# K, V, dK and dV transfers with token blocks dealt to the partitions 16 apart: what it does to a decode-attention forward and backward kernel

## The chip, the cores and the metric

The kernel runs on one core of a Trainium2 chip. The metric is the device time of one execution in microseconds (us). A run is labelled slow when it takes over 1.5% longer than the fastest run of the same kernel beside it, else fast; a kernel run only once has no label. Ratios below are the mean time of one kernel's fast runs over that of the other kernel's fast runs of the same rounds, so they are not quite the ratio of the medians that are quoted.

## The reference

One decode step of a conditioned block, with its gradients. The part that costs time is attention of one query over caches of 32 heads, 8192 tokens and 192 channels:

```python
scores = einsum('bhqd,bhkd->bhqk', q, k) * Dh ** -0.5    # k, v: (1, 32, 8192, 192), bfloat16
p = softmax(scores)
o = einsum('bhqk,bhkd->bhqd', p, v)
# then an output product and a small MLP; jax.vjp of it all returns
# dK and dV (each as large as K) and the smaller gradients
```

K, V, dK and dV are 100 MB each. Softmax and the sums over tokens do not care which token is where, as long as K, V, dK and dV agree.

## The kernel before

A head's 8192 tokens are spread over 128 partitions, 64 neighbouring tokens (a block of 24 KB in DRAM) to each. A transfer moves half a block per partition: 128 runs of 12,288 contiguous bytes, 1.5 MB.

```python
K_hd = [A_k_cache[0, h].rearrange("(p j) d -> p j d", p=P) for h in range(HQ)]   # P = 128, j = 64 tokens
# ... V_hd, dK_hd and dV_hd likewise

def load_k(h, t):                       # t: first or second half of each block; JH = 32
    kb = KB[(2 * h + t) % NKB]
    nc.sync.dma_start(out=kb, in_=K_hd[h][:, t * JH : (t + 1) * JH, :])
    return kb
# ... load_v is the same for V, issued from the same queue

def store(dst, s, src, lo=0, hi=JH):    # dV and dK, issued from the GpSimd queue
    h, t = ht(s)
    nc.gpsimd.dma_start(out=dst[h][:, t * JH + lo : t * JH + hi, :], in_=src[:, lo:hi, :])
```

There are two long stages. In the first, K and V of all heads are read for the forward pass. In the second, V is read again and dV and dK are written. Buffers let transfers run a few ahead of the compute.

## Time and profile before

| | before |
|---|---|
| time, median of 3 runs | 1442.29 us |
| first stage, up to the issue of the first dV store | 605.4 us |
| second stage, from there to the end | 840.5 us |
| load packets of 12,288 B, first stage: median, mean | 464, 481 ns |
| the same, second stage | 460, 485 ns |
| store packets of 12,288 B: median, mean | 460, 467 ns |

The packet rows come from the trace's record of every DMA packet. (Throughout, packets count as first stage from 50 us up to the first large store packet.) The stages are cut at the first start of the store line. The trace's view of it gives the least, median and longest duration in ns, then the first and the last start in us; the span (below) less 605.4 is the second stage.

```profile
L1113 POOL DMA_DIRECT2D out_dram<-KB x131: 531/533/590, 605.4 to 1432.6; - x131
```

The page of the kernel before gives the DMA engines by slices of one fortieth of the span: the mean busy share of the 16 DMA engines in tenths, and the GB/s that they moved.

```profile
span 1445.9 us, 30125 instructions
...
DMA  9999999999999996399999999999999999999997
GB/s 376 415 411 417 402 417 407 402 390 408 402 398 393 417 390 247 115 326 422 410 426 415 424 414 409 401 420 426 411 426 425 422 415 414 409 387 412 413 399 321
```

DMA is full except for a dip between the stages. The table by stretches of the kernel before, one stretch inside each stage. After the stretch and its length come the busy times (with the number of instructions in brackets) of TensorE, its weight loads, VectorE, ScalarE and GpSimd, then TensorE's granted clock, the DMA share and GB/s.

```profile
100.00:500.00 400.00, 368.48 (x5355) 283.78 (x5353) 378.44 (x353) 292.07 (x927) 6.46 (x12) 0.99 1.00 405
700.00:1400.00 700.00, 575.32 (x4280) 323.77 (x4277) 487.75 (x695) 413.56 (x580) 107.64 (x188) 0.55 1.01 414
```

In the first stage VectorE is busy 378 of 400 us while DMA is full (share 1.00): the two are balanced. Waits of the kernel before (us in total, times, longest):

```profile
DVE KB L882 <- DMA out_dram<-KB: 18.8, 10, 3.6
...
DVE prod L298 <- DMA KB<-in_A_k_cache_dram: 5.4, 2, 4.9
```

VectorE hardly waits for DMA. But there is no reserve: in the first stage a K load lands a median of about 1 us before its first use (worked out from landing and first reader). The DMA issues of the kernel before (count, size of each, median us from issue to landing):

```profile
out_dram<-KB POOLq DMA_DIRECT2D x125, 1536.0 KB, 15.8
VB<-in_A_v_cache_dram SPq DMA_DIRECT2D x123, 1536.0 KB, 11.4
KB<-in_A_k_cache_dram SPq DMA_DIRECT2D x64, 1536.0 KB, 10.2
```

### The profile page before, as it was taken

How to read it: one execution, taken by the hardware profiler on the slowest of the kernel's cores; microseconds unless marked ns; L12 is line 12 of the kernel's file. 1: busy time of each engine (PE TensorE's matmuls, PEld its weight loads, DVE VectorE, ACT ScalarE, POOL GpSimd, SP SyncE). 2: the span in 40 equal slices, each digit the busy share in tenths (PEclk: the TensorE clock that was granted, in tenths of full speed). 3: DMA queues.
4: the chain of work that ended last, by engine and by line, in shares of the span. 5: the costliest groups of instructions: out<-in, count | busy, mean ns of one | idle time of the engine just before them, and what ended most of it. 6: DMA issues, size and time to landing. Idle time of an engine off the chain costs nothing.

```text
span 1445.9 us, 30125 instructions
## 1 busy us (share of the span) xinstructions
PE 1213.8 (84%) x12639; PEld 793.1 (55%) x12639; DVE 1112.4 (77%) x1377; ACT 894.5 (62%) x1955; POOL 142.7 (10%) x256
## 2 busy tenths in 40 slices
PE   3899999999999989878888888889788878778874
PEld 1677777677777668644444444444444444444532
DVE  5999999999999986667676667676776667677674
ACT  0777767677777774555566565566565565555654
POOL 0000000000000000112111111111111011111111
PEclk8999999999999998565565555565555555555555
DMA  9999999999999996399999999999999999999997
GB/s 376 415 411 417 402 417 407 402 390 408 402 398 393 417 390 247 115 326 422 410 426 415 424 414 409 401 420 426 411 426 425 422 415 414 409 387 412 413 399 321
DMA packets 77703, 569.35 MB, mean 394 GB/s; under 512 B 8798, under 2 KB 26542, under 8 KB 37502
## 3 DMA queue, kind: packets, MB, share of 16 engines
q1 hardware_dynamic: 50842, 340.44, 58.7%
q0 software_dynamic: 26704, 226.97, 37.8%
q8 instruction: 99, 1.62, 0.4%
q14 instruction: 38, 0.31, 0.1%
q10 hardware_dynamic: 20, 0.00, 0.0%
HBM read 340.95 MB, written 226.43 MB: 392 GB/s over the span
## 4 chain that ended last, share of the span: by engine, by line
PE 32%; DVE 10%; DMA 6%; ACT 5%; issue 4%; POOL 1%; ACTq 0%; POOLq 0%; DVEq 0%
PE dot_ps L866 19%; DMA out_dram<-KB 6%; PE dv_ps L877 6%; DVE pq L857 5%; PE wT_ps L742 4%; ACT KB L878 2%; ACT wT L743 2%; DVE KB L882 1%; DVE dP L313 1%; PE do_ps L756 1%; DVE dq_junk L989 1%; ACT v_bc L961 0%; DVE dS L1161 0%; ACT do_r L757 0%; POOL er_b L700 0%
## 5 line engine op out<-in xcount | busy, mean ns | idle before, releaser
L878 ACT CAST KB<-dv_ps 128x768 bf16<-128x768 f32 x512 | 388.8, 804 | 275.6 <-PE dv_ps L877 273.1
L866 PE MATMUL dot_ps<-pq,ident_bf 128*128 128x256 bf16 x1536 | 365.2, 408 | 57.2 <-DVE pq L857 57.1
L357 ACT ACTIVATE vs<-VB,Ef 128x192 bf16<-128x192 bf16 x872 | 314.5, 442 | 0.0
L866 PEld LDWEIGHTS <-ident_bf 128*128 128x128 bf16 x1536 | 190.5, 135 | 185.7 <-issue 122.5
L877 PE MATMUL dv_ps<-do_r,er_b 1*128 1x192 bf16 x2048 | 222.3, 337 | 55.1 <-ACT KB L878 53.6
L882 DVE TENSOR_TENSOR KB<-qs_bc,dS 128x3072 bf16<-128x3072 bf16 x128 | 224.2, 1753 | 25.8 <-DMA out_dram<-KB 18.8
L857 DVE TENSOR_TENSOR pq<-VB,do_r 128x3072 bf16<-128x3072 bf16 x126 | 220.7, 1751 | 0.0
L298 DVE TENSOR_TENSOR prod<-KB,qs_bc 128x6144 bf16<-128x6144 bf16 x62 | 207.8, 3352 | 11.3 <-DMA KB<-in_A_k_cache_dram 5.4
L372 PE MATMUL mp<-vs,KB 128*128 128x193 bf16 x1984 | 194.3, 251 | 0.0
L877 PEld LDWEIGHTS <-er_b 1*128 1x128 bf16 x2048 | 92.2, 111 | 177.9 <-issue 173.7
L372 PEld LDWEIGHTS <-KB 128*128 128x128 bf16 x1984 | 174.6, 100 | 18.8 <-issue 4.5
L313 DVE TENSOR_REDUCE dP<-dot_ps 128x32 f32<-128x512 f32 x64 | 44.2, 691 | 145.4 <-PE dot_ps L866 145.4
L309 PE MATMUL dot_ps<-prod,ident_bf 128*128 128x512 bf16 x372 | 94.3, 391 | 44.2 <-DVE prod L303 44.2
L350 DVE TENSOR_TENSOR vs<-VB,E 128x1728 bf16<-128x1728 bf16 (+1 forms) x122 | 127.1, 1063 | 0.0
L303 DVE TENSOR_TENSOR prod<-prod 128x3072 bf16<-128x3072 bf16 x62 | 108.6, 1752 | 0.6
L377 PE MATMUL mp<-vs,KB 128*64 128x193 bf16 x1984 | 107.7, 252 | 0.0
L743 ACT COPY wT<-wT_ps 128x1024 bf16<-128x1024 bf16 x84 | 80.8, 962 | 43.0 <-PE wT_ps L742 42.8
L700 POOL DMA_DIRECT2D er_b<-eT_d x64 | 36.9, 577 | 590.1 <-PE dv_ps L877 579.2
L377 PEld LDWEIGHTS <-KB 128*64 128x64 bf16 x1984 | 80.7, 110 | 19.9 <-issue 19.9
L309 PEld LDWEIGHTS <-ident_bf 128*128 128x128 bf16 x372 | 34.8, 99 | 85.8 <-issue 57.8
L1113 POOL DMA_DIRECT2D out_dram<-KB x131 | 70.4, 542 | 46.4 <-ACT KB L878 38.5
L337 ACT ACTIVATE E<-S_h,negm 128x256 bf16<-128x256 f32 x31 | 15.7, 508 | 90.1 <-DVE negm L496 86.4
(269 smaller groups left out, 1005.0 us busy)
## 6 DMA issues: line engine op xcount, KB each, us to landing
out_dram<-KB POOLq DMA_DIRECT2D x125, 1536.0 KB, 15.8
VB<-in_A_v_cache_dram SPq DMA_DIRECT2D x123, 1536.0 KB, 11.4
KB<-in_A_k_cache_dram SPq DMA_DIRECT2D x64, 1536.0 KB, 10.2
wo_st<-in_A_wo_dram SPq DMA_DIRECT2D x31, 480.0 KB, 10.5
w_st<-in_A_wq_dram SPq DMA_DIRECT2D x12, 960.0 KB, 16.1
out_dram<-wo_st POOLq DMA_DIRECT2D x16, 480.0 KB, 19.0
out_dram<-w_st POOLq DMA_DIRECT2D x7, 960.0 KB, 17.7
w_st<-in_w_mod_dram SPq DMA_DIRECT2D x6, 960.0 KB, 15.2
```

Source lines behind the costliest of these rows:

```text
L298: V_.tensor_tensor(out=prod, in0=src, in1=vec[:, None, :].to_broadcast([P, JH, DH]), op=ALU.mult)
L309: T_.matmul(ps, lhsT=ident_bf, rhs=prod[:, :, k : k + TS], start=(k == 0), stop=(k == w - TS))
L350: V_.tensor_tensor(out=vs[:, 0:n, 0:DH].rearrange("p j (a b) -> p j a b", b=4), in0=v[:, v0 : v0 + n, :].rearrange("p j (a b) -> p j a b", ...
L357: A_.activation(out=vs[:, k, 0:DH], in_=v[:, v0 + k, :], func=ACT.Copy, scale=Ef[:, j0 + k : j0 + k + 1])
L372: T_.matmul(mp[:, 0:MW], lhsT=kb[:, j0 + k, 0:P], rhs=vs[:, k, 0:MW], start=(q == 0 and k == 0), stop=(z and k == JQ - 1), skip_group_chec ...
L377: T_.matmul(mp[p0 : p0 + 64, MO : MO + MW], lhsT=kb[:, j0 + k, P:DH], rhs=vs[:, k, 0:MW], start=False, stop=(z and k >= JQ - 2), skip_grou ...
L743: A_.copy(out=wT[:, x0 * P : (x0 + n) * P], in_=tp[:, 0 : n * P])
L857: V_.tensor_tensor(out=pq[:, q], in0=v_l[s][:, q * JQ : (q + 1) * JQ, :], in1=do_of(ht(s)[0])[:, None, :].to_broadcast([P, JQ, DH]), op=AL ...
L866: T_.matmul(ps[:, q * JQ : (q + 1) * JQ, :], lhsT=ident_bf, rhs=pq[:, q, :, k : k + TS], start=(k == 0), stop=(k == DH - TS), skip_group_c ...
L877: T_.matmul(ps[:, b, k * DH : (k + 1) * DH], lhsT=er[p0 : p0 + 1, 2 * m + k, :], rhs=doh[p0 : p0 + 1, :], start=True, stop=True)
L878: A_.copy(out=dV4[:, 2 * q : 2 * q + 2, m * PW : (m + 1) * PW], in_=ps[:, :, 0:PW])
L882: V_.tensor_tensor(out=dK[:, lo:hi, :].rearrange("p j (a b) -> p j a b", b=4), in0=qh.rearrange("p (a b) -> p a b", b=4)[:, None, :, :].to ...
```

## The change

Its intent: blocks of DRAM that are read (or written) at one moment should be neighbours, not far apart. (Which blocks are under way together no trace shows: its packet records name no engine and no partition.) Partition p = 8u + v now holds block 16v + u. The core of the diff (it defines `hd` twice, with no effect):

```diff
-    K_hd = [A_k_cache[0, h].rearrange("(p j) d -> p j d", p=P) for h in range(HQ)]
-    (V_hd, dK_hd, dV_hd likewise)
+    def hd(x):
+        return [x[0, h].rearrange("(v u j) d -> u v j d", v=8, u=16) for h in range(HQ)]
+
+    K_hd, V_hd, dK_hd, dV_hd = hd(A_k_cache), hd(A_v_cache), hd(out_2), hd(out_3)
...
-        nc.sync.dma_start(out=v, in_=V_hd[h][:, t * JH : (t + 1) * JH, :])
+        nc.sync.dma_start(out=v, in_=V_hd[h][:, :, t * JH : (t + 1) * JH, :])
(load_k and store likewise)
```

A K load's DRAM side, written [step, count] in elements, goes from `[[12288, 128], [1, 6144]]` to `[[12288, 16], [196608, 8], [1, 6144]]`. Its SBUF side stays 128 partitions. Bytes, runs of 12,288 bytes and the number of instructions stay the same.

More of the change, by code (lines that the diff above doesn't have):

```diff
@@ L198, with hd @@
     dwm_v = out_9.rearrange("(i p) n -> p i n", p=P)
-    K_hd = [A_k_cache[0, h].rearrange("(p j) d -> p j d", p=P) for h in range(HQ)]
-    V_hd = [A_v_cache[0, h].rearrange("(p j) d -> p j d", p=P) for h in range(HQ)]
-    dK_hd = [out_2[0, h].rearrange("(p j) d -> p j d", p=P) for h in range(HQ)]
-    dV_hd = [out_3[0, h].rearrange("(p j) d -> p j d", p=P) for h in range(HQ)]
+    def hd(x):
+        return [x[0, h].rearrange("(v u j) d -> u v j d", v=8, u=16) for h in range(HQ)]
+    K_hd, V_hd, dK_hd, dV_hd = hd(A_k_cache), hd(A_v_cache), hd(out_2), hd(out_3)
+    def hd(x):
+        return [x[0, h].rearrange("(v u j) d -> u v j d", v=8, u=16) for h in range(HQ)]
+    K_hd, V_hd, dK_hd, dV_hd = hd(A_k_cache), hd(A_v_cache), hd(out_2), hd(out_3)
     def load_w(view3, lo, hi):
@@ L331, in load_k @@
             kb = KB[(2 * h + t) % NKB]
-            nc.sync.dma_start(out=kb, in_=K_hd[h][:, t * JH : (t + 1) * JH, :])
+            nc.sync.dma_start(out=kb, in_=K_hd[h][:, :, t * JH : (t + 1) * JH, :])
             return kb
@@ L1112, in store @@
         h, t = ht(s)
-        nc.gpsimd.dma_start(out=dst[h][:, t * JH + lo : t * JH + hi, :], in_=src[:, lo:hi, :])
+        nc.gpsimd.dma_start(out=dst[h][:, :, t * JH + lo : t * JH + hi, :], in_=src[:, lo:hi, :])
     def dv_gen():
```

## The prediction

> What bounds the kernel now. Two long stages, and the DMA engines are full in both. The table by stretches gives a DMA share of 1.00 with 401 to 411 GB/s from 100 to 500 us (K and V are read) and 1.00 to 1.01 with 402 to 420 GB/s from 700 to 1400 us (V is read, dV and dK are written). VectorE is almost as full in the first (94 of every 100 us); in the second TensorE is (81 to 85, at a granted clock of 0.52 to 0.57). The stages are balanced: from 100 to 540 us the view of waits shows VectorE waiting 0.4 us for a K load, yet a K load lands only 0.1 to 2.5 us (median 1.1) before its use, worked out from issue, landing and first reader. In the second stage a V load lands mostly some 20 us early (the least 1.9), and VectorE waits 18.8 us in all for stores to free a buffer; the chain that ended last gives 6% to those stores.
>
> What the change does. No byte, instruction or packet size changes: still 12,288 contiguous bytes per partition. Only the DRAM block behind each partition changes, from p to 16*(p mod 8) + p div 8, for loads and stores alike, so results stay right. The outermost DRAM dimension becomes 16 instead of 128.
>
> Gain to be had. In the packet records of 12,288 bytes the loads of the first stage have a median of 464 ns, those of the second and the stores 460; the shortest are 460, which is 16 x 12,288 B / 460 ns = 427 GB/s. So 95% of them already run at the floor. Only the tail (5 to 7% of the load packets and 2% of the store packets above 500 ns, up to 2 us) could be DRAM conflict. Its excess over 462 ns, shared over 16 engines, is 17 us in the first stage and 9.5 (loads) + 5.7 (stores) us in the second. The first 17 us are mostly hidden under VectorE. If the whole tail went I would expect 5 to 20 us less. A gain above 2% (29 us) would need more than there is.
>
> The risk. [...] No run here shows it yet. The sign: packets well above 460 ns[...]. Since both stages have no slack in DMA, that would come through nearly whole: an estimate of 1600 to 2000 us. I give this about one chance in three. A few per cent of longer packets from a new DRAM pattern is a smaller risk.
>
> Prediction. Most likely nothing to speak of: 1445 us, with 1425 to 1750 as the range. Faster by over 2%: 0.08; within 2%: 0.52; slower by over 2%: 0.40.
>
> Signs. Right: median packet stays at 460 to 464 ns, GB/s by stretches within 3%, DMA share about 1.0, VectorE still 94 of 100 us in the first stage. If the tail shrinks (mean load packet below 470 ns) without the time falling, the gain was hidden under VectorE and TensorE. Slower: VectorE idles before its K product for the K load, store latency rises from 16 us, GB/s falls at DMA share 1.0.
>
> What would make it wrong: the tail being the pacing of all 16 engines of a transfer (one slow packet delays the landing)[...].

The forecast came to 1445 us, with 1425 to 1750 us as the range and 0.40 for slower by over 2%.

## The result, and the profile after

The changed kernel is correct and slower: 1952.83 us median of 4 runs (1926.06 to 1981.32), against 1442.68 before in the same rounds. The ratio of the fast runs is 1.335, with a 95% interval of 1.327 to 1.343. Two of the four runs were labelled slow, the profiled one among them. Their granted clocks (0.679 and 0.670) are those of the fast ones (0.677 and 0.674). A repeat (below, all four runs labelled fast) took 1978 to 2003 us, and its profile has the same first stage to 0.1 us. So the profile shown here stands for the slower pair and for the repeat; none of a 1926 us run exists.

| | before | after |
|---|---|---|
| first stage | 605.4 us | 1025.2 us |
| second stage | 840.5 us | 954.3 us |
| load packets, first stage: median, mean | 464, 481 ns | 874, 857 ns |
| load packets, second stage: median, mean | 460, 485 ns | 479, 558 ns |
| store packets: median, mean | 460, 467 ns | 460, 531 ns |

Of the 534 us between the profiled spans, 420 us came in the first stage and 114 us in the second. The line of the stores, which cuts the stages, and the page of the changed kernel:

```profile
L1117 POOL DMA_DIRECT2D out_dram<-KB x131: 522/532/717, 1025.2 to 1962.3; - x131
```

```profile
span 1979.5 us, 30125 instructions
...
DMA  9999999999999999999849999999999999999998
GB/s 233 228 226 229 230 234 252 250 238 235 214 219 215 224 218 231 230 223 232 217 127 344 363 374 342 372 365 352 371 376 364 372 365 345 322 366 359 377 362 308
```

The DMA engines are as busy as before, with hardly more than half the bytes per second through the first stage. Here the busy share says nothing of the rate: it is 1.01 at 229 GB/s below, and was 1.00 at 405 GB/s before. The table by stretches of the changed kernel:

```profile
100.00:900.00 800.00, 512.78 (x6048) 370.77 (x6047) 424.46 (x392) 325.18 (x1030) 7.20 (x13) 0.79 1.01 229
1100.00:1900.00 800.00, 580.08 (x4291) 328.76 (x4289) 484.81 (x690) 416.89 (x583) 108.19 (x188) 0.54 1.00 362
```

VectorE now works 424 of 800 us in the first stage, at a DMA share of 1.01; DMA alone sets the pace. The waits of the changed kernel show where that surfaces:

```profile
DVE prod L302 <- DMA KB<-in_A_k_cache_dram: 366.3, 54, 9.5
...
DVE KB L886 <- DMA out_dram<-KB: 146.3, 34, 11.5
```

VectorE waits 366.3 us for K loads, against 5.4, and 146.3 us for stores to free their buffers, against 18.8. The first accounts for most of the 420 us. The DMA issues of the changed kernel:

```profile
out_dram<-KB POOLq DMA_DIRECT2D x125, 1536.0 KB, 21.4
VB<-in_A_v_cache_dram SPq DMA_DIRECT2D x123, 1536.0 KB, 26.7
KB<-in_A_k_cache_dram SPq DMA_DIRECT2D x64, 1536.0 KB, 29.7
```

A K load takes nearly three times as long to land. What is left to explain is why one packet of 12,288 bytes takes 857 ns in place of 481. It is not that fewer packets are under way: counted from their starts and durations, exactly 16 are in flight for 78% of the time from 100 to 500 us before, and for 76% after.

### The profile page after: what moved, and what is told of

Same layout as the page of the kernel before. It is cut to its first block, busy times and chain, and to the rows that moved or that the text cites. A ratio compares the mean times of both kernels' runs of the same rounds, so it can differ in the third digit from the quotient of the medians.

```text
span 1979.5 us, 30125 instructions
## 1 busy us (share of the span) xinstructions
PE 1317.4 (67%) x12639; PEld 846.3 (43%) x12639; DVE 1119.0 (57%) x1377; ACT 895.7 (45%) x1955; POOL 143.6 (7%) x256
## 5 line engine op out<-in xcount | busy, mean ns | idle before, releaser
L302 DVE TENSOR_TENSOR prod<-KB,qs_bc 128x6144 bf16<-128x6144 bf16 x62 | 208.2, 3358 | 404.2 <-DMA KB<-in_A_k_cache_dram 366.3
L870 PE MATMUL dot_ps<-pq,ident_bf 128*128 128x256 bf16 x1536 | 357.5, 401 | 108.8 <-DVE pq L861 108.4
L313 PE MATMUL dot_ps<-prod,ident_bf 128*128 128x512 bf16 x372 | 150.6, 568 | 302.9 <-DVE prod L307 302.9
L886 DVE TENSOR_TENSOR KB<-qs_bc,dS 128x3072 bf16<-128x3072 bf16 x128 | 224.2, 1752 | 152.4 <-DMA out_dram<-KB 146.3
L870 PEld LDWEIGHTS <-ident_bf 128*128 128x128 bf16 x1536 | 187.8, 133 | 234.5 <-issue 173.8
L376 PE MATMUL mp<-vs,KB 128*128 128x193 bf16 x1984 | 238.0, 285 | 0.0
L376 PEld LDWEIGHTS <-KB 128*128 128x128 bf16 x1984 | 212.3, 116 | 38.4 <-issue 27.6
L861 DVE TENSOR_TENSOR pq<-VB,do_r 128x3072 bf16<-128x3072 bf16 x126 | 220.5, 1750 | 14.1 <-DMA VB<-in_A_v_cache_dram 14.1
L313 PEld LDWEIGHTS <-ident_bf 128*128 128x128 bf16 x372 | 45.8, 125 | 371.9 <-issue 365.0
L381 PE MATMUL mp<-vs,KB 128*64 128x193 bf16 x1984 | 112.2, 259 | 0.0
L381 PEld LDWEIGHTS <-KB 128*64 128x64 bf16 x1984 | 84.7, 114 | 22.7 <-issue 22.7
L429 POOL DMA_DIRECT2D eT_d<-er x16 | 8.8, 551 | 991.8 <-ACT er L428 762.1
## 6 DMA issues: line engine op xcount, KB each, us to landing
out_dram<-KB POOLq DMA_DIRECT2D x125, 1536.0 KB, 21.4
```

The costliest lines, as they stand in the source:

```text
L302: V_.tensor_tensor(out=prod, in0=src, in1=vec[:, None, :].to_broadcast([P, JH, DH]), op=ALU.mult)
L313: T_.matmul(ps, lhsT=ident_bf, rhs=prod[:, :, k : k + TS], start=(k == 0), stop=(k == w - TS))
L376: T_.matmul(mp[:, 0:MW], lhsT=kb[:, j0 + k, 0:P], rhs=vs[:, k, 0:MW], start=(q == 0 and k == 0), stop=(z and k == JQ - 1), skip_group_chec ...
L381: T_.matmul(mp[p0 : p0 + 64, MO : MO + MW], lhsT=kb[:, j0 + k, P:DH], rhs=vs[:, k, 0:MW], start=False, stop=(z and k >= JQ - 2), skip_grou ...
L861: V_.tensor_tensor(out=pq[:, q], in0=v_l[s][:, q * JQ : (q + 1) * JQ, :], in1=do_of(ht(s)[0])[:, None, :].to_broadcast([P, JQ, DH]), op=AL ...
L870: T_.matmul(ps[:, q * JQ : (q + 1) * JQ, :], lhsT=ident_bf, rhs=pq[:, q, :, k : k + TS], start=(k == 0), stop=(k == DH - TS), skip_group_c ...
```

## The experiments

Theory P (partitions): the loss comes from how a transfer is dealt out over the partitions, wherever its blocks lie in DRAM; 16 as outermost DRAM dimension brings it on, and so do loads that cover only part of the partitions. Theory D (DRAM): blocks that neighbour each other conflict in DRAM when they are read at the same time. Two smaller rivals come up below. All edits are to the kernel before, and the diffs are shortened; fast runs of the kernel before took 1440 to 1458 us beside them.

### Far apart in DRAM, but 16 outermost

```diff
+ rearrange("(u t v j) d -> u v t j d", u=16, t=2, v=8)   # K, V, dK, dV
+ load: in_=K_hd[h][:, :, t, :, :]   # pitch of u 192 KB, 96 KB in one piece for each u
```

> The DRAM access of K, V, dK and dV keeps 16 as outermost dimension[...]. Theory P[...]: as slow as the changed kernel, 1850 to 2000 us, load packets of 12,288 bytes at 800 to 930 ns in the first stage. Theory D (blocks that neighbour each other in DRAM and are read at the same time conflict there): as the kernel before, 1430 to 1480 us, packets at 460 to 480 ns.

Measured: 1974.42 us (one run), first-stage load packets 850 ns in the mean. In its table by stretches:

```profile
100.00:900.00 800.00, 510.65 (x6060) 367.73 (x6059) 432.92 (x398) 329.00 (x1043) 7.20 (x13) 0.78 1.01 233
```

Each u now has its eight blocks in one piece, and the pieces of neighbouring u begin 192 KB apart, as the change wanted to avoid. The loss is whole, at the 1850 to 2000 us of theory P; theory D had 1430 to 1480.

### Neighbours in DRAM, but 32 or 64 outermost

```diff
+ rearrange("(v u j) d -> u v j d", v=4, u=32)    # and, in another run, v=2, u=64
```

> [...]the outermost DRAM dimension is 32, each entry being a group of four partitions. Theory P: [...]the time is that of the kernel before, 1430 to 1480 us with packets of 460 to 480 ns; if it needs 128 entries, as slow as the changed kernel. Theory D: slow, 1800 to 2000 us.

> As the run with 32 outermost, with 64 groups of two partitions instead. Theory P: [...]1435 to 1455 us with packets at 460 to 480 ns. If 32 was fast only because a group of four is one entry, 64 may be slow (over 1800 us).

Measured with 32: 1445.26 us (one run), first-stage load packets 480 ns. With 64: 1446.98 us median of 4, ratio 0.999 (0.993 to 1.005), 480 ns. The tables by stretches with 32 and with 64:

```profile
100.00:500.00 400.00, 367.65 (x5364) 283.46 (x5363) 379.38 (x353) 292.90 (x929) 6.47 (x12) 0.99 1.00 406
```

```profile
100.00:500.00 400.00, 367.30 (x5360) 283.16 (x5357) 378.70 (x353) 292.64 (x928) 6.48 (x12) 0.99 1.00 405
```

This is the change's order in DRAM, with neighbouring u again one block apart, without its loss and without any gain. Theory D had 1800 to 2000 us for the run with 32. The step that costs lies between 32 entries in the outermost dimension (480 ns a packet) and 16 (857 ns), that is between groups of 4 and of 8 partitions. Why it lies there no run shows.

### The whole transfer in one piece of DRAM

```diff
+ rearrange("(t p j) d -> p t j d", p=P, t=2)
+ load: in_=K_hd[h][:, t, :, :]      # 128 outermost, blocks of 12 KB, 1.5 MB contiguous
```

> The outermost dimension stays 128, but each transfer of 1.5 MB is one contiguous piece of DRAM: blocks of 12 KB, one after the other over the partitions.[...] Theory P: [...]1425 to 1450 us, packets at 460 to 470 ns; if the tail of slow packets came from DRAM it may shrink and give up to 15 us. Theory D: slower than before, over 1600 us.

Measured: 1451.53 us median of 4, ratio 1.002 (0.997 to 1.007), just above the expected range and the same as before within the noise. First-stage load packets 480 ns; 5.1% of them over 500 ns, against 5.5% before. So the tail of slow packets did not shrink with this spacing either, and the hoped-for gain of up to 15 us is not there. Theory D had over 1600 us. Its table by stretches:

```profile
100.00:500.00 400.00, 368.40 (x5379) 284.23 (x5376) 378.42 (x354) 290.37 (x921) 6.46 (x12) 0.99 1.00 405
```

### The kernel before with loads of fewer partitions

A positive control, that is an edit that should bring on the same loss by another way: DRAM blocks and stores of the kernel before, but a load covers only part of the partitions at a time.

```diff
-        nc.sync.dma_start(out=v, in_=V_hd[h][:, t * JH : (t + 1) * JH, :])
+        for p0 in (0, 64):           # other runs: range(0, P, 32) and range(0, P, 16)
+            nc.sync.dma_start(out=v[p0 : p0 + 64], in_=V_hd[h][p0 : p0 + 64, t * JH : (t + 1) * JH, :])
```

> The kernel before with each K and V load cut into two of 64 partitions (0 to 63, then 64 to 127); DRAM blocks, their spacing and the contiguous 12,288 bytes per partition are untouched, stores too. Theory P: [...]load packets go to 700 to 930 ns and the first stage to 800 to 1000 us, like the changed kernel; the whole 1750 to 1950 us. Theory D: packets at 460 to 480 ns, within 2% of the kernel before.

> As the run with halves, with each K and V load cut into four of 32 partitions. Theory P[...] no worse than the halves: first-stage packets 800 to 950 ns, first store at 1000 to 1080 us. Rival S (what costs is that a DMA is cut into smaller ones or covers fewer partitions): about twice the halves, packets or gaps between them making the first stage 1500 us or more.

> As the run with halves, with each K and V load cut into eight of 16 partitions[...]. Theory P[...] packets[...] 1400 to 1900 ns[...], and a first stage of 1700 to 2200 us[...]. [...]as the halves, about 1040 us.

The last words, "as the halves, about 1040 us", are the other case: loads of 16 partitions lose no more than those of 64.

| partitions in one load | time, one run | first stage | load packets, first stage, mean |
|---|---|---|---|
| 128 (kernel before) | 1442 us | 605.4 us | 481 ns |
| 64 | 1939.95 us | 1037.7 us | 867 ns |
| 32 | 1951.88 us | 1048.7 us | 873 ns |
| 16 | 2282.53 us | 1351.6 us | 1151 ns |

The same stretch in the halves, in the quarters, and a like one in the eighths:

```profile
100.00:900.00 800.00, 511.36 (x5952) 368.34 (x5950) 422.81 (x389) 325.08 (x1030) 7.16 (x13) 0.76 1.01 227
```

```profile
100.00:900.00 800.00, 506.75 (x5947) 363.79 (x5946) 417.24 (x385) 325.18 (x1030) 7.16 (x13) 0.78 1.01 225
```

```profile
100.00:1200.00 1100.00, 539.72 (x6160) 385.19 (x6160) 443.08 (x404) 337.78 (x1068) 7.15 (x13) 0.70 1.00 172
```

Halves reproduce the changed kernel's first stage almost exactly (867 against 857 ns) with the DRAM layout untouched. Theory D had 460 to 480 ns here. It has missed its figures in all four layouts in which it was tried (16 far apart, 32 outermost, one piece, halves) and falls. Quarters cost no more than halves (873 against 867 ns), although their loads are half as large; rival S, by which cutting or narrowing a load is the cost, had a first stage of 1500 us or more for them, and 1048.7 was measured. Eighths cost more again, 1151 ns. So packets do not get slower in proportion as a load covers fewer partitions. What is left is theory P in the form above: every layout tried with 16 outermost or with loads of part of the partitions lost. Why 64 and 32 partitions cost the same and 16 more is not shown: no run compares sets of one size chosen in another way. The first stage of the halves came out above its expected 800 to 1000 us. The eighths missed the expected 1400 to 1900 ns and the first stage of 1700 to 2200 us: 1151 ns and 1351.6 us were measured, between these and the other case.

### Loads alone, stores alone

```diff
+ loads:  rearrange("(v u j) d -> u v j d", v=8, u=16); stores as before     (first run)
+ stores: rearrange("(v u j) d -> u v j d", v=8, u=16); loads as before      (second run)
```

Both give wrong rows in dK, since loads and stores then disagree about the tokens.

> Only the K and V loads get the changed access, dK and dV are stored as before (so the rows of dK and dV land permuted: a wrong result on purpose). Theory P with most of the cost in the loads: the first stage as in the changed kernel (first store at about 1030 us), load packets at 800 to 930 ns there; the second stage between the two kernels, 860 to 920 us; the whole 1860 to 1960 us. If the stores carry the cost: near 1450 us.

> Only the dK and dV stores get the changed access, K and V are loaded as before (rows permuted again: wrong on purpose). If the stores, which are issued from another engine than the loads, are split over the engines in the same way: store packets above 500 ns in 15 to 25% of cases against 3% before, the second stage longer by 30 to 100 us, the whole 1470 to 1550 us. [...]within 1% of the kernel before, and the slow store packets of the changed kernel came from its loads.

In the second expectation, "within 1% of the kernel before" is the case in which the changed access costs the stores nothing.

| changed access on | time | first stage | second stage | store packets, mean |
|---|---|---|---|---|
| nothing (before) | 1442 us | 605.4 us | 840.5 us | 467 ns |
| loads | 1898.16 (fast), 1937.83 (slow, profiled) | 1037.5 us | 898.6 us | 481 ns |
| stores | 1567.42 us, ratio 1.083 | 602.7 us | 965.0 us | 564 ns |
| both (the change) | 1952.83 us | 1025.2 us | 954.3 us | 531 ns |

Both queues suffer; the stores issued from GpSimd are no exception (564 against 467 ns, with the stores alone changed). The second stage and the waits with the stores alone:

```profile
700.00:1400.00 700.00, 509.07 (x3747) 286.83 (x3746) 426.92 (x620) 363.17 (x508) 95.21 (x166) 0.54 0.99 362
```

```profile
DVE KB L885 <- DMA out_dram<-KB: 146.4, 28, 12.3
```

For store buffers VectorE waits about as long as in the changed kernel (146 us). As expected, 24% of the store packets took over 500 ns; the second stage's 124 us and the whole were more than expected (30 to 100 us, 1470 to 1550 us). In these profiles the second stage loses 58 us by the loads and 124 us by the stores, but 114 us by both together, so here the two losses do not add. The profiles of loads and of both are of runs labelled slow, with faster runs of the same kernels 40 and 55 us shorter. Why the two do not add was not tried.

### A shorter issue path

The compiled program marks the K and V loads of the kernel before for a shorter issue on the queue's sequencer: 0.33 us each, against 0.54 us for the K loads of the changed kernel, which have no mark. Rival Q: loads without the mark are carried out more slowly. The mark was switched off in the kernel before.

```diff
+    nc.dge_precook = False
```

> The kernel before, with the mark removed by which the compiler gives its loads a shorter issue (0.33 us each; the changed kernel's K loads have no such mark and take 0.54 us). Theory P: loads take 0.54 us to issue but packets stay at 460 to 480 ns, and the time stays within 1% of the kernel before. Rival Q (loads without the mark are carried out in another, slower way): 1800 us or more with packets above 800 ns.

The issues of K loads before, in the changed kernel and with the mark off (again least, median and longest in ns):

```profile
L332 SPq DMA_DIRECT2D KB<-in_A_k_cache_dram x64: 327/328/3602, 2.8 to 540.4; - x64
```

```profile
L336 SPq DMA_DIRECT2D KB<-in_A_k_cache_dram x64: 536/537/6724, 2.8 to 939.9; - x64
```

```profile
L332 SPq DMA_DIRECT2D KB<-in_A_k_cache_dram x64: 471/472/3698, 4.3 to 541.9; - x64
```

Measured: 1448.89 us median of 2, ratio 1.001 (0.994 to 1.008), packets 481 ns. A K load took 0.47 us to issue, not the expected 0.54; the rest may belong to the extra dimension. Rival Q falls. The runs with 32 and 64 outermost say the same: their K loads have no mark and have the extra dimension, and they lost nothing (480 ns a packet).

### The changed kernel again

> The changed kernel once more, because its profiled run was one of the slower ones (1981 against 1926 us) at the same granted clock. Expected: 1920 to 1985 us, load packets of the first stage at 830 to 880 ns. [...]the mean load packet of a faster run is shorter in one of the stages.

Measured: 1985.68 us median of 4 (1977.87 to 2003.04), ratio 1.370 (1.359 to 1.381) to the kernel before in the same rounds. First stage 1025.2 us, second 962.9 us, first-stage load packets 860 ns. Two of the runs (1990 and 2003 us) are above the expected 1985 us, and since none came near 1926 us, whether a faster run has shorter packets was not answered. The changed kernel's runs spread from 1926 to 2003 us over both sets of rounds at about one clock (0.656 to 0.679); the kernel before stays within 1440 to 1458. No profile of a 1926 us run exists, so where its 50 us less lie stays open.

## Why the prediction was wrong

- **What bounds the kernel.** Right: DMA was full in both stages (shares 1.00 and 1.01). The first-stage packets grew by 857/481 = 1.78 and the stage by 1025.2/605.4 = 1.69, so the cost came through nearly whole. In the second stage the growth of the packets' means, over 7,560 load and 16,000 store packets and shared by 16 engines, is an estimate of 99 us, and 114 were lost.
- **The gain to be had.** Right in kind: no gain hidden in the tail, or in DRAM spacing, was found. Three layouts with very different spacing (32, 64 and 128 outermost) all stay within 0.3% of the kernel before.
- **The risk.** That 16 outermost entries could cost was right, and in the first stage so was the size: "1600 to 2000 us" was estimated and 1953 measured; packets "well above 460 ns", and 857 measured. In the second stage packets grew far less (558 and 531 ns).
- **The step that failed** is the cost of a packet under "most likely nothing to speak of": no packet size changes, so the "median packet stays at 460 to 464 ns". That took 16 outermost entries to be as good as 128. The packets did not stay there: a first-stage load packet took 874 ns in the median (857 in the mean), and the stage 1025 us in place of 605, while 32 and 64 entries kept 480 ns in the mean. The risk had been given only "about one chance in three", and the upper end of 1750 us left most of its own estimate outside. The author's argument that it should have been the leading case rested on rules that no trace of this case shows, and is left out. The trace of the kernel before could not decide it: all its K, V, dK and dV transfers have 128 outermost. The step from 480 to 857 ns was first seen in the runs.
- **Signs.** The slow signs came as listed: VectorE idle before its K product for the K load (5.4 to 366.3 us), store latency up (15.8 to 21.4 us), GB/s down (405 to 229) at a DMA share of 1.0.
- **What stays open.** The packet records name no engine and no partition, so what makes a packet take longer is not seen. The runs show that 16 outermost entries (857 ns) and loads of 64 partitions (867 ns) cost nearly alike; that the two have one cause is not shown. Why the same access costs so much less per packet in the second stage (558 ns for loads, 531 for stores) is open too.

## What to carry to other kernels

Keep the outermost dimension of the DRAM side of a 128-partition transfer at 128; 64 and 32 were as good here (480 ns a packet), and 16 (857 ns) cost a third of the run time at an unchanged DMA busy share (1.01). If token or row blocks are to be dealt out in another order, put the regrouping into inner dimensions or into groups of two or four partitions, the cases that cost nothing here. When DMA is full, look at the duration of packets of one size before looking at DRAM: a median of 460 to 464 ns next to the shortest of about 460 for 12,288 bytes said at once that DRAM spacing had next to nothing to give.
